# A DeltaNet and MLP-mixer kernel: its steps in another order of issue

## The chip, the cores and the metric

The kernel runs on one NeuronCore of a Trainium2 chip. Its time is the device time of one launch in microseconds (us), from first to last work on that core. Several runs are taken and their median is given; one further execution is recorded by the hardware profiler, and its trace and page are what is read here. Engines are named as the profile names them: PE is the matrix engine (TensorE), PEld its weight load, DVE the vector engine, ACT the scalar engine, POOL is GpSimd, SP the engine that issues the DMAs.

## The reference

Inputs are q, k, v of shape (4, 8, 768, 48), beta (4, 8, 768), and four weight matrices. A recurrence over 768 steps comes first, then an MLP-mixer on its outcome. All is float32.

```
k_n = k / (norm(k, axis=-1) + 1e-6)
for t in range(S):                                  # per batch and head
    y[t]  = q[t] @ state                            # state is 48 x 48
    state = state + beta[t] * outer(k_n[t], v[t] - k_n[t] @ state)
x = y as (B, S, H * D)                              # (4, 768, 384)
h   = relu(x^T @ w_tok1) @ w_tok2                   # 768 -> 256 -> 768, over tokens
u   = x + h^T
out = u + relu(u @ w_ch1) @ w_ch2                   # 384 -> 1536 -> 384, over channels
```

## The kernel before

The recurrence is computed in chunks. A *unit* u is 128 tokens of one batch for all eight heads: 24 units, six to a batch. A *chunk* t is 64 tokens: 48 chunks, twelve to a batch. Inside a chunk the steps become products of matrices, for which a triangular matrix has to be inverted; from chunk to chunk a state of 48 x 48 for each head is handed on, so the chunks of a batch must follow each other. A mixer needs all twelve chunks of its batch.

The work is written as Python generators, each of which issues a few instructions and then yields. One `next` of a generator is called a *step*. The jobs are:

- `k{u}` loads k and q of a unit (`load_kq`, L296): one DMA for k (kpad), one for q (qpad), and either four copies on ACT (first four units) or four more DMAs (`stacked`, L315) for a second layout of k (kst).
- `v{u}` loads v in four DMAs (v_st) and scales it on POOL (L328).
- `p{u}` prepares a unit (`prep`, L344): norms of k, transposes on PE (L376, L392), products p_g (L406), masking by DVE into gm (L412). Its last steps (`to_parts`, L465) hand the unit's triangular blocks to the inversion: by copies on chip for the first six units, by four DMAs into DRAM (n_dram, L479) for the others.
- `i{rnd}` inverts the blocks of two to four units at once (`invert`, L501): units 0 to 3 are round 0, units 4 and 5 round 1, then four at a time and two in round 6. It is a chain of pairs of DVE instructions (L523 a product into sub, L528 the addition to x). From round 2 on x is read from DRAM in its first step (L517) and written to it in its last (w_dram).
- `f{u}` brings the inverted blocks back to gm (`from_parts`, L484).
- `h{u}` (`join_16`, L547; first six units only) and `j{u}` (`join`, L578) put the small inverted blocks together, with PE, ACT and DVE by turns. In `join_16` the four last copies alternate between ACT and DVE (L574).
- `r{t}` is a chunk of the recurrence: `recur_early` (L605) for batch 0, `recur` (L681) for the others. It goes from PE to DVE (L630 or L703, the subtraction of v, into rw_bd), back to PE (p_w), to ACT, to PE (p_s), and DVE writes the next state (L657 or L733, s_bd).
- `m{b}` is the mixer of a batch (L752): p_1 and p_h for the tokens, then in pairs of units p_c (L821) with a relu on ACT (L828), and seven products p_o (L841), each added to the residual xb by DVE (L790). L814 forms sums that save one of eight products.
- `w{j}` loads a piece of a weight matrix and rounds it (`round_weights`, L206) with DVE, ACT and POOL by turns (L221, L226, L233, L235).
- `b` loads beta. `x`, `z` (`keep_warm`, L162) and `y` (`warm_tiles`, L171) are matmuls of zeros that nothing reads.

There is no scheduler: `tc.manual_schedule()` leaves instructions as they are recorded, and the string `order` in the kernel lists 2148 steps by job, `p4*3` being three steps of p4. Each engine gets its instructions in that sequence, and works through them in it; an instruction waits on semaphores for what it reads and for buffers that come free. SP takes DMA issues in the same way. PSUM is shared by three groups of buffers: prep (two), seq (two), mlp (three). v_st has two buffers, kpad and qpad four each, gm room for six units.

The loop at the end of the kernel:

```
for word in order.split():
    name, _, n = word.partition("*")
    for _ in range(int(n or 1)):
        next(jobs[name])
```

Of the kernel before, what the change touches and what calls it, by code (L numbers as in the profile page):

```python
# [10 lines left out]
ALU = mybir.AluOpType  # L11
# [12 lines left out]
def kernel(  # L24
# [39 lines left out]
    nc = tc.nc  # L64
# [56 lines left out]
    for i in range(2):  # L121
        r = slice(C * i, C * i + C)
# [5 lines left out]
    NV = 6  # L128
# [6 lines left out]
    kqts = tiles("kqt", [128, NB, 2, C], NV)  # L135
# [4 lines left out]
    r_bd = w_bd = const.tile([128, NP, 2 * D], FP32, name="rw_bd")  # L140
# [12 lines left out]
    w1 = const.tile([128, NCH, DTOK], FP32, name="w1")  # L153
    w2 = const.tile([128, NDH, S], FP32, name="w2")
# [113 lines left out]
    vsts = {}  # L268
    ksts = {}
    rounds = [[0, 1, 2, 3], [4, 5]]  # L270
    while rounds[-1][-1] < NU - 1:
        u = rounds[-1][-1] + 1
# [68 lines left out]
    def gm_of(u):  # L341
        return gmb[:, (u % NV) * NB : (u % NV + 1) * NB]
# [88 lines left out]
    for n in (QB * RU * NB, RU * NB * QB):  # L431
# [5 lines left out]
        out=low16,  # L437
        in_=ident.rearrange("s (q t) -> s q t", t=HB)[:, :, QB:HB],
# [242 lines left out]
    def recur(t):  # L681


        b, c = divmod(t, NQ)
        u, cc = divmod(t, 2)
        assert t == len(steps)
        steps.append(t)
        gm, kqt, v_st = gm_of(u), kqts[u % NV], vsts[u]
        if c == 0:
            xbs[b] = mlp_pool.tile([128, NCH, DM], FP32, name="xb", tag="xb")  # L690
        y = xbs[b][C * cc : C * cc + C, c // 2].rearrange("s (p n) -> s p n", p=NP)
# [4 lines left out]
        if c > 0:  # L696
            p_q = ps_seq([128, NP, 2 * D], "p_q")
            for p in range(NP):
                nc.tensor.matmul(p_q[:, p], kqt[:, 2 * p + cc], s0[:, p])  # L699
            yield  # L700
            for i in range(2):
                r = PAR[i ^ cc]
                nc.vector.tensor_tensor(  # L703
                    out=r_bd[r, :, ends[i ^ cc]], in0=p_q[lo, :, ends[i]],
                    in1=v_st[r, :, cc], op=ALU.subtract,
                )
        else:
            for r, e in zip(PAR, ends):
                nc.gpsimd.tensor_copy(out=r_bd[r, :, e], in_=v_st[r, :, cc])
        yield  # L710

        assert u in scaled and u in joined
# [194 lines left out]
    jobs["z"] = keep_warm(4)  # L907
    jobs["y"] = jobs["Y"] = warm_tiles()
    order = """
    k0 b y w10 y x k0*5 y*2 w10*3 p0*3 b*2 w1*3 k1*2 p0*2 w10 p0 w1 p0*3 x*2 p0 k1*4  # L910
    p1 w3 x w3*3 v1 w1 p0 k2 v1 k2*2 k3 x*3 p1*2 k2 v1 p0 k2 p0 k2 p1*2 p2*2 k3 v0*2
    p1*4 z x p1 x p2*3 k3*3 p1 k4 v1 w6 k3 w3 p0*2 p1*2 k4 p2*4 v0 k4 y*2 p3*2 p0 w6
    p1 p2*4 p3*4 y*2 w6 y k4*2 p4 p3 v0 p4 k5*2 w2 k5 p1 p3*2 p4 p2*4 p1 y*2 p1 k5*2
    p3*6 p0 p3*2 i0*2 v0 z k6 k7 k6 i0 k5 p4*2 i0*2 k6*2 w6 i0 k4 w6 w2 i0 w2 i0 y
    w18*2 v1 i0 z y*3 x p4*4 y*2 p4 x*2 p4*2 z x*2 y*3 k8 x z x*3 k7*4 k8 z*3 k8*4
    i0*3 w8 p4 i0*4 p5 w2 k6 w2 i0 w18 w13 w8 p5 p4*3 y*3 h0*2 k7 f0*2 w18 f0 p5 f0
    p5 h1*2 z p6 h2*2 f2*2 p5 h0*4 j0 h0 y*2 p5 f2*2 x p6 w18 k6 w8 p4 j0*2 p5*3
    h2*5 j0*2 y*2 w8 r0*2 f1*4 w8 w13*2 p5*4 r0*3 h1*2 r0 h1 p5*3 h1 p5 h1 w13 x*2
    r1*2 y*2 r1*2 p7 r1 h3 k9 w11 k9 w11 j1*2 i1 k9*2 i1 w11 w0 i1 r1 j2 r1 h3 z i1
    j1*2 r1 w11 f3 w11 v2 i1 j1 r2*2 j2*2 i1 r2 p7 w0 p6*4 w0 r2*2 y j2*2 r1 i1 r2*2  # L920
    f3*2 p8 f3 x*3 r2*2 r3*2 i1 w13 v2 r3 x r3*2 x w5 i1 v2 k9 w5 i1 w0*2 h3 v2 p6*2
    h3 p6*2 w5 r3 y v2 r3*3 h3*3 y*2 k9 w5 k10 i1*2 j3 r4 k10 p6 w14*2 r4 w14*2 w5
    p8 p6 r4*2 i1 w14 r4 w17*2 y p7 r4 j3 p8 i1 w17 y w17 y*2 j3 r4*3 k10*2 p6 r5 i1
    r5*2 j3*2 w17 w9*2 i1 p7 r5*2 i1 p7*2 w16 v4 w16 v4 p6 w9 p7*4 v4*2 y w16 r5*3
    y*2 z r5 v3 v4 v3*2 w9 v3 k11 p6*2 p9 p7 v3 p7*2 r6*3 p8 w9 h4*2 r6 w16 r6 p6
    w27*2 w16 p8*3 w27 k11 p8 w7 r6 p8 r6*2 f4 r6 p9*2 h5*2 x f4 p9 r7*2 w7*2 p8
    w27*2 r7 k12 k10 f4 p10 f5 p8 w7 p8*2 f5*2 r7 f4 z p7 f5 w24*2 p9*2 y*3 p7 w24
    h4 r7*2 v5 p7*2 p8 w26 w7 p9*2 z w4 h4 w24 h4*2 r7*2 h4 p10 p9 p10 p9 w24 w26*3
    p8 j4 p9*3 y w4*2 p8 y r7 x j4*2 w26 p10 h5*4 r8*2 j4 v5 w28 v5 y k13 j4 h5 j5
    r8*3 y*2 p9*4 w28 w27 w28 p8 w4 r8 p10 r8 w29 r8*2 w4 w28 w29 r9*3 j5 w29 v5 r9  # L930
    i2 y i2 y i2 w28 i2 r9*4 k11*2 v5 i2*2 j5*2 r10 j5 r10 k12 i2 z r10*2 k13 y k11
    y r9 k13 w15*2 i2 w15 k13 v7 w22 p11 w29*2 r10*4 y*3 r10 p10*2 i2 w22 i2 w22 i2
    r11 y k11 y k13*2 y*2 k12 y*2 k10 r11*3 k12 i2 w15*2 i2*2 w22 w19*2 w22 r11 v7*3
    i2 w19 k12 i2 w12*2 i2 w12 i2 v6 i2 z w19*2 w12*2 r11*2 m0*3 p10*2 w21 v6*3 w23
    i2*5 m0*3 z m0 i2*2 m0 i2 m0*2 i2*2 m0*4 x p10 w25*2 i2*2 w25 i2 p11 w21*2 w25*2
    w31 p11 w23 z w23 w21*2 w23 f7 f6 w31*2 f6*3 f9 k12 f7 f9 w23 v6 v7 m0*2 w31 m0
    f7 m0*2 j6 w31 p12 m0*3 w20 f8 j6 f8*3 j6 m0 j6*2 r12 m0 r12 w29 p12*2 j7 w25 j7
    p13 f7 w20 p11*2 j8 r12*2 j7 f9 j7 p11 w20*2 j8 k14 f9 k14 j7 j8 w25 r12 w20 x
    r13 p10 r13*2 p10*2 r13 w32 w27 w32*2 m0 j9 w32 r13*2 w32 m0 r14 p12*3 m0 p10*4
    v8*2 j8*2 r14*2 p11 w30 j9 w23 p11 r14*2 j9 m0*2 w30 p11 v8 w30 p11 w30 j9*2 r14  # L940
    w30 r15 k14*2 p13 r15 w29 p11*3 k14 k16 r15*2 v8 m0 k16 k14 p12*3 w33 w25 w33
    w27 m0 r15 w33 k16 p12 k16 p11*2 p13 p12 p11 r15 v10 k15*5 p12 v10*2 v8 w33 m0
    w23 r16 p12 w33 p12 v10 p12*3 p13 m0 p11 k16 p13*5 r16 w23 w31 m0 w29 w31 w33*2
    r16 p14 p13*4 w33 p13*4 w31 i3 r16*3 m0*3 p14*2 r17*2 p14 m0*2 v9*2 m0 i3*2
    p14*2 i3 v9*2 i3 r17 p14 k17*2 i3*3 m0*2 k17*2 m0 i3*2 p14 m0 v9 r17*2 i3*3 r17
    v10 p15*2 m0 i3*2 p14*2 i3*2 m0 k17 k18 i3*4 p15 p16 m0*5 r18 m0*2 i3 m0*3 r18
    m0 i3 m0*4 i3*2 k15 i3*3 r18*2 k18*2 p14 k18*2 i3*4 r18*2 m0*5 r19*2 f10*4 m0
    f11*2 p14*5 m0 v11*2 r19 k16 m0 p16*2 j10 m0*2 f13 v11 f11 p15*2 f12 f13 r19*3
    j10 m0 j10 m0*2 p17*2 j11 p15*4 r20*2 p15 j10 f12*2 j10 j11 k19*2 m0 p16 r20 p18
    j11 p18 k17 v11 f11 r20 j12 p15*2 v11 r20*2 m0 r21 j11 p15 j12 j11 p14 j12 f13  # L950
    r21*2 p16 m0 r21 p15*2 k19 p15*2 v12*5 r21 p17 p16*2 k19 p16 p17 r21 m0*2 r22*2
    p16 p18 p16*3 r22 f13 k19*2 p16 p18 p16*2 f12 r22 p16 m0*2 r22*2 m0*3 r23*2
    p17*5 m0 j12*2 r23*2 k21*2 m0 v13 r23 p17*3 v13 p17 v13*2 r23 j13 p16 v13 m0*4
    k21*2 k20*3 k21*2 p17*2 k20 p17*2 m0*2 k18 m0*5 k20 i4*2 m0*2 i4*2 k20 i4*2 m0
    i4*2 m0*2 i4 p18 j13 i4*2 r24*2 p20 r24 m1 r24*2 m1 i4*3 r25*2 i4 v14 p18 i4*2
    m1*2 p18*3 m1 i4*3 m1 j13*2 r25 m1 j13 r25*2 i4 r25 m1*2 i4*3 m1 v14*3 m1 r26*2
    p20 m1*3 r26*2 p18*2 i4*3 v14 i4 p19*3 p18 i4*3 k22 i4 m1 r26 f15 f14*2 r26
    f16*2 f15 f14 k22*2 f17 p20 m1*3 r27 p20 r27 p19 j14 m1 p19 p18 m1*8 p19 m1*4
    j14 f15*2 k22 r27 p18*2 k22 j15 f17*2 j14 v15*2 k22 f14 r27 m1*2 r27*2 j14*2 j15
    r28*2 m1*2 j15 f16 f17 r28 j15 m1 r28*3 p19*2 m1 j16 v15*2 j15 r29*2 p19*3 r29  # L960
    p19*2 m1 p20 r29*2 p22 r29 j16 m1 r30 j16 k23*3 p18 j17 p22 p18 f16 p19*2 m1*2
    p20*2 v15 p20*2 r30*3 v16*2 j16 p21*2 j17 r30*2 p21 j17 v16*3 m1*2 r31 p19 k23*2
    p21 p20 j16 p20 r31*3 p23 p20 v17*4 p20*2 m1 p21 m1 p20*3 p23 p21*2 r31*2 p21*2
    v17 p23*2 m1 p21 r32 p22*2 p21 m1*2 p21*4 p19 p21*2 j17 r32*2 m1 r32*3 k23 m1
    r33*2 m1*2 r33*2 i5 p22*2 j17 m1 r33 i5 m1 i5*3 r33 i5 m1*2 i5*4 p22*2 i5*2 p22
    m1*2 p22 i5 v18*5 m1*3 r34*2 i5*2 p22 m1*2 p22 r34 i5*2 m1*2 i5 p23 r34 m1 r34
    i5 r34 i5 m1*2 i5*2 m1*3 i5*3 p22*5 i5 m1*2 i5*6 m1 f18*4 f19*4 r35*2 f21 v19
    m1*5 f21 m1*4 f21*2 j18 m1 j18 p23 j18 r35*2 m1*5 p23 v19 m1 p23 r35 j18 p23 j19
    f20 j19 f20 m1 f20 m1*2 j19 m1*8 j20 m1 j18 v19 r36*3 p23*6 r36*2 p23*2 r35 m2*2
    r37 i6 r37 i6*5 m2*4 r37 v20 m2 i6 r37 f20 r37*2 v20*2 v19 v20 m2*2 i6*2 m2 i6  # L970
    m2*2 i6 v19 m2*2 r38 j20 j19*2 m2 r38*3 m2 j21 i6 r38 i6*3 m2 r38 i6 j20 r39*2
    m2*2 i6*2 r39 i6*3 v21 r39 v21*2 i6*2 m2 r39 j20*2 m2 i6*2 v21 i6*2 j21*2 i6 v20
    i6*2 r39 i6*2 m2*10 r40*2 f23 m2 f23*2 f22 m2 r40*2 f22*2 m2 v21 m2*3 r40*2 f23
    m2*2 r41 j21*2 f22 j22*2 r41*3 v22 m2*3 r41 j23 v22 m2*3 r41 m2*16 r42 m2*2 j22
    r42*2 m2*2 r42*3 m2*2 v22*3 r43*2 j22 j23 r43 m2*2 r43*3 v23 m2*2 r44*2 j22
    v23*4 m2 j23*2 r44*2 m2*2 r44*2 m2 r45 j23 m2 r45*2 m2 r45*3 m2*2 r46*2 m2 r46
    m2 m3 r46*3 m3 r47*2 m2*2 r47*2 m3 m2 m3 r47*2 m3 m2 m3*2 m2*3 m3*4 m2 m3 m2*3
    m3 m2*4 m3 m2*6 m3*88 x
    """
    for word in order.split():  # L980
        name, _, n = word.partition("*")
# [34 lines left out]
```

## Time and profile before

| | us |
|---|---|
| median of five runs | 722.23 (715.38 to 725.86) |
| the profiled execution | 717.61 |
| its span, first to last instruction | 715.8 |
| PE busy | 688.2 (96%) |
| weight load busy | 600.3 (84%) |
| DVE busy | 438.2 (61%) |
| ACT busy | 242.0 (34%) |
| POOL busy | 98.0 (14%) |

The page cuts the span into 40 slices of 17.9 us and gives the busy share of each engine in tenths (9 is 90% or more), and the granted PE clock in tenths:

```profile
PE   8699898999999999999999999999999999999998
PEld 6468777757889999987999898978999986989987
DVE  6987989798899974568555695258723332221212
ACT  7546656424652324213244312113212231021110
POOL 2221353223231012200012100000000000000000
PEclk9987999799999999999999999999999999999999
```

A float32 matmul of the program shows as two records in the trace, a transpose as one. Matmuls overlap each other in the trace, so the sum of their lengths says less than the distance from the start of one to the start of the next. "Idle before" in the list of groups is the time in which the engine had nothing to run ahead of an instruction; a wait is put down to what came last.

### The profile page before, as it was taken

The page shows a single profiled execution, that of the slowest core. Times are in us where ns is not written, and L with a number is a line of the kernel's source. Part 1 is how long each engine was busy: PE and PEld are TensorE (multiplying, and loading weights), DVE is VectorE, ACT ScalarE, POOL GpSimd, SP SyncE. Part 2 cuts the span into 40 slices and gives each one's busy share as a digit, 9 for nine tenths or more (in the row PEclk, how much of TensorE's full clock was granted, in tenths as well). Part 3 has the DMA queues.
Part 4 walks back from the last instruction along what each step waited for, and adds up shares of the span by engine and source line. Part 5 has one row for each costly group of instructions (what it writes and reads, how often), then busy time and mean ns, then how long its engine had stood idle before and what let it go on. Part 6 is the DMA issues. An engine that isn't in the chain of part 4 may idle for free.

```text
span 715.8 us, 18631 instructions
## 1 busy us (share of the span) xinstructions
PE 688.2 (96%) x7784; PEld 600.3 (84%) x7784; DVE 438.2 (61%) x1163; ACT 242.0 (34%) x569; POOL 98.0 (14%) x118
## 2 busy tenths in 40 slices
PE   8699898999999999999999999999999999999998
PEld 6468777757889999987999898978999986989987
DVE  6987989798899974568555695258723332221212
ACT  7546656424652324213244312113212231021110
POOL 2221353223231012200012100000000000000000
PEclk9987999799999999999999999999999999999999
DMA  9752465843554244431322203020110100000000
GB/s 182 154 114 56 101 147 128 172 125 81 119 105 95 35 100 74 79 79 24 74 47 60 65 1 82 12 64 12 31 34 1 34 1 1 23 0 23 1 23 22
DMA packets 146756, 46.14 MB, mean 64 GB/s; under 512 B 138064, under 2 KB 141136, under 8 KB 146672
## 3 DMA queue, kind: packets, MB, share of 16 engines
q1 hardware_dynamic: 146672, 44.95, 28.8%
q8 instruction: 61, 1.00, 0.6%
q14 instruction: 23, 0.19, 0.1%
HBM read 35.49 MB, written 9.44 MB: 63 GB/s over the span
## 4 chain that ended last, share of the span: by engine, by line
PE 76%; DVE 12%; DMA 5%; SPq 3%; issue 2%; ACT 1%; DVEq 0%; ACTq 0%
PE p_c L821 25%; PE p_o L841 21%; PE p_q L699 4%; PE p_s L725 4%; PE p_w L715 4%; PE p_h L772 3%; PE p L759 3%; PE p_g L406 3%; PE p_x L598 2%; DVE x L528 2%; PE p_warm L166 2%; DMA x<-n_dram 2%; PE p_z L589 1%; DVE sub L523 1%; DMA d<-in_moe_w_ch_dram 1%
## 5 line engine op out<-in xcount | busy, mean ns | idle before, releaser
L821 PE MATMUL p_c<-u_t,wc 128*128 128x256 f32 x864 | 196.4, 381 | 0.0
L821 PEld LDWEIGHTS p_c<-u_t,wc 128*128 128x128 f32 x864 | 160.7, 190 | 21.7 <-issue 0.5
L841 PE MATMUL p_o<-wc,r 128*128 128x192 f32 x720 | 126.7, 328 | 1.5 <-DVE xb L790 0.9
L841 PEld LDWEIGHTS p_o<-wc,r 128*128 128x128 f32 x720 | 117.1, 190 | 3.5 <-DVE xb L790 1.2
L828 ACT ACTIVATE r<-p_c 128x512 f32<-128x512 f32 x72 | 42.8, 596 | 184.9 <-PE p_c L821 184.9
L790 DVE TENSOR_TENSOR xb<-xb,p_o 128x192 f32<-128x192 f32 x84 | 29.4, 350 | 75.0 <-PE p_o L841 75.0
L523 DVE TENSOR_TENSOR sub<-x 128x84 f32<-128x84 f32 (+24 forms) x178 | 59.1, 332 | 12.3 <-DMA x<-n_dram 8.6
L528 DVE TENSOR_TENSOR x<-x,sub 128x84 f32<-128x84 f32 (+24 forms) x178 | 62.6, 352 | 6.1
L814 DVE TENSOR_TENSOR s<-r 128x384 f32<-128x384 f32 x24 | 13.7, 570 | 74.1 <-ACT r L828 74.1
L841 PE MATMUL p_o<-wc,s 128*128 128x192 f32 x288 | 50.7, 327 | 0.0
L233 POOL TENSOR_TENSOR w_f<-w_f,d 128x384 uint32<-128x384 uint32 (+1 forms) x34 | 34.0, 1000 | 115.8 <-DVE w_f L226 52.5
L841 PEld LDWEIGHTS p_o<-wc,s 128*128 128x128 f32 x288 | 46.8, 190 | 0.0
L718 ACT COPY rw_bd<-p_w 64x192 f32<-64x192 f32 x72 | 22.4, 311 | 54.5 <-PE p_w L715 53.0
L328 POOL TENSOR_TENSOR v_st<-v_st,nrm 128x384 f32<-128x384 f32 x24 | 20.9, 875 | 144.4 <-DMA v_st<-in_v_dram 53.2
L412 DVE TENSOR_TENSOR gm<-p_g,mb 128x512 f32<-128x512 f32 x48 | 31.3, 683 | 12.6 <-POOL gm L397 6.1
L385 POOL TENSOR_TENSOR mb<-mask_c,cs 128x512 f32<-128x512 f32 x20 | 21.5, 1073 | 125.5 <-DVE gm L412 67.7
L699 PEld LDWEIGHTS p_q<-s_bd,kqt 128*128 128x128 f32 x264 | 33.6, 191 | 3.7 <-issue 1.2
L699 PE MATMUL p_q<-s_bd,kqt 128*128 128x96 f32 x264 | 34.3, 273 | 1.5 <-DVE s_bd L733 1.5
L725 PEld LDWEIGHTS p_s<-rw_bd,gm 128*112 128x112 f32 x288 | 33.0, 178 | 3.0 <-issue 0.5
L703 DVE TENSOR_TENSOR rw_bd<-p_q,v_st 64x192 f32<-64x192 f32 x66 | 23.1, 350 | 20.2 <-PE p_q L699 15.1
L759 PE MATMUL p<-xb,w 128*128 128x384 f32 x96 | 34.6, 501 | 0.0
L725 PE MATMUL p_s<-rw_bd,gm 128*112 128x96 f32 x288 | 34.2, 262 | 0.0
(111 smaller groups left out, 965.6 us busy)
## 6 DMA issues: line engine op xcount, KB each, us to landing
d<-in_moe_w_ch_dram SPq DMA_DIRECT2D x24, 384.0 KB, 3.6
kpad<-in_k_dram SPq DMA_DIRECT2D x24, 192.0 KB, 3.5
qpad<-in_q_dram SPq DMA_DIRECT2D x24, 192.0 KB, 3.7
v_st<-in_v_dram SPq DMA_DIRECT2D x96, 48.0 KB, 2.6
out_dram<-xb SPq DMA_DIRECT2D x24, 192.0 KB, 1.9
kst<-in_k_dram SPq DMA_DIRECT2D x80, 48.0 KB, 2.8
n_dram<-gm SPq DMA_DIRECT2D x72, 32.0 KB, 1.8
gm<-w_dram SPq DMA_DIRECT2D x72, 32.0 KB, 2.1
```

Source lines behind the costliest of these rows:

```text
L233: nc.gpsimd.tensor_tensor(out=f, in0=f, in1=lo, op=ALU.add)
L412: nc.vector.tensor_tensor(out=blocks(gm)[:, :, cc, 0 : 2 * C].rearrange("s p (two n) -> s p two n", two=2), in0=p_g[cc], in1=mb[:, :, cc, ...
L523: nc.vector.tensor_tensor(out=tmp, in0=y[:, :, 0:s, s : s + 1].to_broadcast([n, k, s, w]), in1=y[:, :, s : s + 1, s + 1 : m].to_broadcast( ...
L528: nc.vector.tensor_tensor(out=y[:, :, 0:s, s + 1 : m], in0=y[:, :, 0:s, s + 1 : m], in1=tmp, op=ALU.add,)
L699: nc.tensor.matmul(p_q[:, p], kqt[:, 2 * p + cc], s0[:, p])
L715: nc.tensor.matmul(p_w[0 : C + 1, p], gm[:, 2 * p + cc, 0 : C + 1], r_bd[:, p])
L725: nc.tensor.matmul(p_s[0 : C + D, p], gm[:, 2 * p + cc, C:], w_bd[:, p])
L759: nc.tensor.matmul(p_1[dh], piece_of(w1, c, 0)[:, dh * 128 : (dh + 1) * 128], xb[:, c], start=(c == 0), stop=(c == NCH - 1),)
L790: nc.vector.tensor_tensor(out=xb[:, c, e], in0=xb[:, c, e], in1=p, op=ALU.add)
L821: nc.tensor.matmul(p_c[:, k], piece_of(wc1, cb, f * 128)[:, f * 128 : (f + 1) * 128], u_t[:, cb], start=(cb == 0), stop=(cb == NCB - 1),)
L828: nc.scalar.activation(r2[:, m], p_c, ACTF.Relu)
L841: nc.tensor.matmul(p, a[:, m], wc2[:, m, j], start=(start and m == 0), stop=(m == NM - 1), skip_group_check=True,)
```

## The change

The string `order` is replaced by another. It has the same steps, and as many of each job, but for one `z` less and one `x` more. Both versions begin in another way, place the loads, preparations and inversions differently among the mixers' steps, and end alike. The description given with it is that the order was searched with both nominal and lengthened operations.

The function `recur` is edited in one thing: it looks up `vsts[u]` where v is used, not at its first step, so that a recurrence's first step may stand ahead of the job that makes v's buffer.

```diff
-        gm, kqt, v_st = gm_of(u), kqts[u % NV], vsts[u]
+        gm, kqt = gm_of(u), kqts[u % NV]
...
-                    in1=v_st[r, :, cc], op=ALU.subtract,
+                    in1=vsts[u][r, :, cc], op=ALU.subtract,
...
-                nc.gpsimd.tensor_copy(out=r_bd[r, :, e], in_=v_st[r, :, cc])
+                nc.gpsimd.tensor_copy(out=r_bd[r, :, e], in_=vsts[u][r, :, cc])
```

From the order, first its beginning, then the stretch from i2's end to r12, the stretches around i3 and i4, those with v16 and v20, and the end:

```diff
-    k0 b y w10 y x k0*5 y*2 w10*3 p0*3 b*2 w1*3 k1*2 p0*2 w10 p0 w1 p0*3 x*2 p0 k1*4
-    p1 w3 x w3*3 v1 w1 p0 k2 v1 k2*2 k3 x*3 p1*2 k2 v1 p0 k2 p0 k2 p1*2 p2*2 k3 v0*2
+    w2*3 w3 y x w3*2 w2 k0 b x w3 k1 v1 x*4 k2 k0*4 x*2 w2 w10 k0 p0 v1 w3 p0 k1*3 y
+    x k1*2 k3 z v1 p1 b p1 p0 b p0*6 p1 w10 x p0 p1 w10 k2*5 p2 p1*2 p0*3 p2 p1*4 z
...
-    i2*5 m0*3 z m0 i2*2 m0 i2 m0*2 i2*2 m0*4 x p10 w25*2 i2*2 w25 i2 p11 w21*2 w25*2
+    v6 m0 v6 p12 m0 i2 m0 i2*2 m0 i2 m0*2 i2 w23 i2 w23 i2 w25*3 i2*2 p10*4 m0*2 z
...
-    r16 p14 p13*4 w33 p13*4 w31 i3 r16*3 m0*3 p14*2 r17*2 p14 m0*2 v9*2 m0 i3*2
-    p14*2 i3 v9*2 i3 r17 p14 k17*2 i3*3 m0*2 k17*2 m0 i3*2 p14 m0 v9 r17*2 i3*3 r17
-    v10 p15*2 m0 i3*2 p14*2 i3*2 m0 k17 k18 i3*4 p15 p16 m0*5 r18 m0*2 i3 m0*3 r18
+    r17*2 i3*2 m0*2 v9*3 r17*2 k16 i3 m0 k16 m0 v10 i3*2 k16 r18*2 v10*3 i3*3 p16*2
+    m0*4 k15 k17 i3*21 k15 k17*2 r18*2 p14 m0*2 i3 m0 f10 r18*2 v10 f10*2 f13 p14*2
...
-    p17*5 m0 j12*2 r23*2 k21*2 m0 v13 r23 p17*3 v13 p17 v13*2 r23 j13 p16 v13 m0*4
-    k21*2 k20*3 k21*2 p17*2 k20 p17*2 m0*2 k18 m0*5 k20 i4*2 m0*2 i4*2 k20 i4*2 m0
+    r23 p17 j13 r23 p16*2 p17 m0*2 v13*5 r23*3 p17*4 p20 m0 j13 k20 k21*2 j12 k21
+    p20 p18 m0 p18 m0 p17 m0*6 p17*3 i4*5 j12 m0 p18 i4 m0*3 i4*2 k21*2 m0*2 i4*3
...
-    p20*2 v15 p20*2 r30*3 v16*2 j16 p21*2 j17 r30*2 p21 j17 v16*3 m1*2 r31 p19 k23*2
+    m1 r30 p19*2 r31*2 p20 v17*3 p20*4 m1 p20 m1 p20 v16 p21*3 j16 r31 j16 r31 p21
+    m1 r31*2 p21*2 v16*2 p20 v16*2 p21*4 r32*2 p21*3 m1*2 i5 j17*2 r32*2 p23*2 m1*2
...
-    m2*2 i6*2 r39 i6*3 v21 r39 v21*2 i6*2 m2 r39 j20*2 m2 i6*2 v21 i6*2 j21*2 i6 v20
+    r39*2 j20 j21 r40 m2 j21 j20 j21*2 v20*2 i6 v20*3 r40*3 m2 i6*4 r40*2 i6 m2 r41
...
-    m3 m2*4 m3 m2*6 m3*88 x
+    m3*17 x*2 m3*71
```

## The prediction

> **What bounds the kernel now.** I first split the profiled execution into stretches. The three lines below give the length of a stretch, the busy time of each engine in it with its instruction count, the granted TensorE clock, and the DMA share and rate.
>
> ```profile
> 0.00:160.00 160.00, 139.07 (x3126) 108.66 (x3127) 135.23 (x358) 89.65 (x220) 47.42 (x60) 0.89 0.60 132
> 160.00:260.00 100.00, 98.37 (x963) 87.30 (x962) 89.93 (x237) 39.61 (x93) 21.43 (x23) 1.00 0.39 86
> 260.00:716.00 456.00, 450.79 (x3698) 404.32 (x3696) 213.05 (x570) 112.74 (x256) 29.18 (x35) 1.00 0.16 36
> ```
>
> The columns after the length are PE, weight load, DVE, ACT, POOL. DVE is busy 85% and 90% in the first two stretches, then 47%. PE looks full throughout, but I don't take its busy time at face value. I charge each matmul the spacing it shows when nothing holds it up. The chain of waits has it: six p_c records in 1.30 us (216 ns each), six p_o records in 0.98 us (163 ns), four p records in 1.32 us (about 323 ns by the median start-to-start). Counted so, 864 p_c records are 186 us, 1008 p_o 164 us, 192 p and p_h 62 us, the later recurrences (p_q, p_w, p_s) 79 us; with preparation, joins and the rest the useful work is **601 us**. The warm-keeping matmuls (lines 166, 176) are 36 us more. So 715.8 - 601 = 114.5 us of the span is lost to PE: 91 before 160 us (69 us of useful work done by then), 8 from 160 to 260, 15 after. An order can only win from these.
>
> What holds PE early is DVE. Its waits in the first 160 us (us in total, times, longest) are few and short:
>
> ```profile
> DVE w_f L221 <- DMA d<-in_moe_w_ch_dram: 5.8, 2, 3.9
> DVE gm L574 <- ACT gm L574: 5.3, 6, 2.6
> DVE s_bd L657 <- PE p_s L653: 2.6, 2, 1.4
> DVE sub L523 <- DMA x<-n_dram: 1.1, 1, 1.1
> ```
>
> Late, a single place stands out, in the chain of waits by time (start, us, what). It is i4, an inversion round whose input goes through DRAM:
>
> ```profile
> 303.39 1.68 DMA n_dram<-gm
> ...
> 305.19 5.41 DMA x<-n_dram
> ...
> 310.63 0.20 DVE sub L523
> ...
> 311.04 0.28 DVE xb L790
> ...
> 311.36 0.76 PE p_o L841 x3
> ```
>
> The step's data goes out and back in 7.2 us; DVE, which takes its instructions in order, stands before it; the residual add xb (L790) behind it frees the PSUM bank that PE needs.
>
> **What the Trainium skill says.** "Perfetto Trace Analysis", Identifying the Most-Contended Engine: matmul busy time is a bad measure since matmuls are pipelined; weight-load busy share is better. The trace agrees: PE is 96% busy but weight load 84%, and p_c's mean record is 381 ns where its spacing is 216. The same page, Optimization Strategy: with regimes of different limits, interleave them. Here PE-heavy m0 can't begin before its recurrences. "TensorE: Matmul & The Clock Gate", Part 1: an array that idles gets a lower clock. The trace shows 0.89 in the first 160 us and 1.00 after, so waits there have a second cost. "DMA: Bandwidth & Descriptors", Anatomy of one DMA: most of a small transfer's fixed time is the completion, worst towards HBM; the 1.7 to 3.2 us of the small n_dram writes fit.
>
> **The change, part by part.** No arithmetic is added or removed: per engine both programs have as many instructions (TensorE 4024, DVE 1163, ACT 569, SP 437, POOL 121). One z becomes an x (warm matmul of 512 columns to one of 128: 0.65 us less, in waits anyway: 0). The late reading of vsts only lets a recurrence's first step stand ahead of its v load: 0 by itself.
>
> *a. DVE's lead.* For every matmul that waits for DVE, I sum DVE's work in program order up to what it waits for (each instruction its median by shape, plus the 34 ns that lie between two of them) and subtract PE's useful work ahead of it. PE has lost at least this, plus DVE's own waits. Where the sum peaks, the front ends. Before: 88.5 us, at r19 (DVE 245.7, PE 157.2). It ran at 256.2 us, so DVE's net waits were 10.5 us and PE's loss 99.0. After: 91.1 us, at r20 (DVE 251.3, PE 160.2). Between, the orders are near-twins: at r0 DVE 54.9 before and 55.4 after, at r11's end 148.7 and 143.6, at i2's end 161.7 and 161.9, at i3's load 206.1 and 207.3, PE within 3 us each time. The later peak comes from r18 to r20 moving ahead of m0 work. **+2.6 us.**
>
> *b. The start.* SP now issues w2, w3, k0, b, k1 and so on, where it issued k0, b, w10, k0's q. Before, DVE's first rounding step waited until 6.1 us: w10's DMA was third, issued at 1.85 us, and took 4.2. Now w2 is first, at about 0.74 us, and should land near 4.6. k0 is third: two issues of 0.43 to 0.6 us later, so its four copies on ACT (from 3.77 us before, 0.36 each) and the square end near 7 to 8 us, beside w2's and w3's rounding on DVE. POOL's w2 and w3 adds fall in POOL's idle time. **-1.5 us** (0 to -2.5).
>
> *c. Round trips through DRAM.* Per round, the time from DVE's last mask product (gm, L412) to the inversion's first DVE step is four SP issues (1.4 us), the write (1.7 to 3.2) and the read (3.5 to 5.7): 6.7 to 10. DVE work placed in between, before and after: i2 15.1 and 9.0, i3 6.1 and 7.8, i4 5.3 and 3.3, i5 4.3 and 3.2, i6 2.1 and 3.3 us. i2's SP queue was held up by two further DMAs before, one now; I take its 1.1 us as gone (bounds -1.1 and +1). i3 had 0.5 us and keeps it. i4 to i6 come when DVE has slack, so PE's cover counts: from the p_g matmul to the first one blocked i4 has 13.8 us after against 13.0, and needs 1.5 + 8.4 + 2.2 = 12.1. Before, two v and k DMAs stood in SP's queue between; these are gone. PE's 1.4 us wait there goes. i5 has 25.9 us; i6 16.7 against at most 16.2. **-1.1 and -1.4 us.**
>
> *d. ACT and POOL.* The join_16 copies (L574) made DVE wait 5.3 us. Pairs that follow each other directly on DVE with ACT's copy between: three before, six now; but fewer stand behind other ACT work. Unknown from the trace: taken as 0, bounds -3 and +3.
>
> *e. v loads moved.* Each must pass SP's queue, land (2.6 us) and be scaled on POOL (0.9 us), about 6 us with its issues. DVE work between the release of the buffer and the use is at least 8 us in all; v16's last issues stand behind p20's write with 3.8 us left, at a place where DVE has 40 us in hand. Cost 0; cover gone, 1 to 2 us of DVE that PE doesn't see.
>
> *f. The tail.* m3's last 71 steps follow alone in both (88 before); 3.6 us from the last matmul to the end of the store stay. 0.
>
> Sum: 717.6 (profiled execution: 715.8 span and 1.8 around it) + 2.6 - 1.5 - 1.1 - 1.4 = 716.2. The median of the five runs, 722.2, stands 4.6 above the profiled one, so the forecast is 716.2 + 4.6, about **720.5 us**.
>
> **Rivals.**
> *Parity* (the forecast): the above; with d and the bounds of b and c, 715 to 727. For it: the twin sums. Chance 0.42.
> *Fewer queue waits, faster*: an order that was laid out for longer operations as well should leave room where the trace shows DVE late although the sum left no gap: L574's 5.3 us, the w_f loads' 5.8, s_bd's 2.6, and 15 us of small PE waits after 260 us. If half of the 13.7 and a third of the 15 go, 720.5 - 6.9 - 5 + 2.6 (b and c not counted twice) = 711. For it: of DVE's waits on other engines that leave under 1 us of room, the orders have 9 and 4 between DVE's 50th and 90th us. Against: from the 200th to the 300th it is 7 and 8. Chance 0.36.
> *DVE falls behind between r17 and r20, slower*: the lead stays above 89 us over 60 us of PE work now, where it touched 88 before; any DVE wait there is paid in full. i3's 21 steps now stand in one row with r18 and the m0 adds behind. If its read takes the 5.7 us that i2's took (round trip 9.8 against 7.8 of cover: +2.0), the L574 pairs cost +3, i2 doesn't gain (+2.1) and b gives nothing (+1.5): 720.5 + 8.6 = 729. It decides once new DVE waits before r20 exceed some 7 us. Chance 0.22.
> That the move changes nothing because PE is full holds only after 260 us, and is part of parity.
>
> **Numbers.** About 1% (7.2 us) is what a measurement of this kernel can tell from no change; its runs spread over 10 us. Range 706 to 732: the fast rival with another 5 us, the slow one with 3 more. Chances: faster by over 1% 0.36, within 1% 0.42, slower 0.22, one for each case.
>
> **What would show it.** a: r19 or r20's p_w near 256 to 260 us, after about 160 us of useful PE work. b: DVE's first w_f step before 5 us. c: no PE stop at i4 and no idle DVE ahead of i2's first step. d: the wait L574 on ACT under 8 us. Wrong, if PE's loss after 260 us departs from 15 us by over 4, or if DVE's waits up to r20 are not 8 to 13 us.

## The result and the profile after

| | before | after |
|---|---|---|
| median, us (lowest to highest; runs) | 721.81 (713.65 to 728.56; 77) | 716.09 (711.09 to 719.77; 42) |
| ratio, 95% interval | | 0.9947 [0.9932, 0.9963] |
| the profiled execution, us | 717.61 | 714.41 |
| its span, us | 715.8 | 712.6 |

The new order is faster by 0.5%, which is less than the 1% taken as "no change". The ratio counts only runs within 1.5% of the fastest of their kernel, which leaves out 29 of before's 77 and none of after's; over all runs the means are 722.04 and 715.79 us, a ratio of 0.991. The new order also spreads less: the standard deviation of its runs is 2.2 us, against 3.8. The profiled executions differ by 3.2 us, the medians by 5.7; before's profiled execution was one of its quicker ones.

First, two lines of the page of after: the busy times, and the group of the inversion's products (columns: busy, mean ns of one, idle time ahead of them and its releaser).

```profile
PE 683.4 (96%) x7784; PEld 595.6 (84%) x7784; DVE 427.1 (60%) x1163; ACT 241.7 (34%) x569; POOL 97.0 (14%) x118
...
L523 DVE TENSOR_TENSOR sub<-x 128x84 f32<-128x84 f32 (+24 forms) x178 | 59.0, 332 | 4.3 <-DMA x<-n_dram 0.3
```

DVE runs the same 1163 instructions and is busy 427.1 us, not 438.2. So the same instructions got shorter, by 11 us in all: something the prediction has no term for. The inversions wait 0.3 us for their DRAM read.

The same three stretches as before, in the same columns:

```profile
0.00:160.00 160.00, 136.19 (x3126) 105.19 (x3127) 131.37 (x365) 90.52 (x221) 47.29 (x61) 0.88 0.61 131
160.00:260.00 100.00, 98.82 (x1098) 88.31 (x1096) 87.02 (x241) 42.90 (x101) 21.19 (x23) 1.00 0.42 91
260.00:713.00 453.00, 448.35 (x3572) 402.06 (x3564) 208.68 (x558) 108.33 (x247) 28.57 (x35) 1.00 0.16 35
```

In the first 160 us DVE finishes 365 instructions in 131.4 us of busy time, where it finished 358 in 135.2. With the prediction's count of useful PE work (601.3 us in both), the loss of PE runs as follows, in us at the given time:

| loss of PE at | 60 | 120 | 160 | 200 | 262 | the end |
|---|---|---|---|---|---|---|
| before | 44.0 | 72.9 | 91.2 | 95.0 | 99.2 | 114.5 |
| after | 42.7 | 70.8 | 86.5 | 93.6 | 96.6 | 111.3 |

Of the 3.2 us, 2.6 are there by 262 us, and 0.6 come later. The time was won in the front, where DVE leads.

Now DVE's waits of after in the first 160 us (us in total, times, longest):

```profile
DVE gm L574 <- ACT gm L574: 7.9, 9, 3.8
DVE s_bd L657 <- PE p_s L653: 3.3, 2, 2.0
DVE w_f L221 <- DMA d<-in_moe_w_tok_dram: 2.3, 2, 1.4
DVE ksum L355 <- ACT ksq L352: 2.3, 2, 1.3
```

They aren't fewer. The w_f loads give back 2.1 us (5.8 to 2.3 and, further down the list, 1.4), but the L574 pairs cost 7.9 us, not 5.3.

To see what DVE's time is made of, I add up its instructions to the subtraction in r19 (L703), where its lead peaked before: each at the median of its shape, then how much longer than that it took ("lengthening"), then the gaps over 60 ns ("waits"). The rest, about -8 us, is the few ns by which each overlaps the next. (r19's p_w, which waits for this subtraction, starts at 256.2 us before and 251.9 after.)

| up to r19's L703, us | ends at | at medians | lengthening | waits |
|---|---|---|---|---|
| before | 255.7 | 224.2 | 17.5 | 21.7 |
| after | 250.2 | 223.6 | 8.2 | 26.5 |

The work is equal, lengthening falls by 9.3 us, waits take 4.8 back, and r19 comes 5.5 us earlier.

What lengthens an instruction shows in the groups by line. The columns are min/median/max ns, first and last start, shape. Before:

```profile
L253 DVE TENSOR_TENSOR wc<-wc x24: 312/350/985, 124.6 to 216.4; 128x192 f32<-128x192 f32 x24
```

```profile
L362 DVE TENSOR_SCALAR nrm<-nrm x24: 129/163/792, 9.2 to 394.4; 128x8 f32<-128x8 f32 x24
```

And after:

```profile
L362 DVE TENSOR_SCALAR nrm<-nrm x24: 120/164/172, 10.3 to 417.6; 128x8 f32<-128x8 f32 x24
```

One shape, one median, and a maximum of three to five times that; in the new order L362 has none. The timeline of before, around the longest L253 (start, us, what):

```profile
204.74 0.95 POOL L328 TENSOR_TENSOR v_st<-v_st,nrm 128x384 f32<-128x384 f32 x1
...
204.92 0.98 DVE L253 TENSOR_TENSOR wc<-wc 128x192 f32<-128x192 f32 x1
```

POOL's product is under way when DVE's subtraction starts. It ends at 205.69, DVE's at 205.90. The Trainium skill says so in "SBUF — State Buffer", Who interferes with whom: a DVE instruction with both inputs in SBUF contends with a GpSimd instruction that reads SBUF, and whichever issues first holds the shared ports for its whole length. The trace agrees: 0.98 us where 0.35 is usual.

### The profile page after: what moved, and what is told of

It reads as the page before. It is cut to its first block, busy times and chain, and to the rows that moved or that the text cites. A ratio compares the mean times of both kernels' runs of the same rounds, so it can differ in the third digit from the quotient of the medians.

```text
span 712.6 us, 18616 instructions
## 1 busy us (share of the span) xinstructions
PE 683.4 (96%) x7784; PEld 595.6 (84%) x7784; DVE 427.1 (60%) x1163; ACT 241.7 (34%) x569; POOL 97.0 (14%) x118
## 4 chain that ended last, share of the span: by engine, by line
PE 76%; DVE 16%; DMA 4%; issue 2%; ACT 2%; SPq 0%; POOL 0%; DVEq 0%; POOLq 0%; ACTq 0%
PE p_c L821 23%; PE p_o L841 21%; PE p L759 5%; PE p_q L699 4%; PE p_s L725 4%; PE p_h L772 4%; PE p_w L715 3%; DVE x L528 3%; DVE sub L523 3%; PE p_x L598 2%; PE p_z L589 2%; PE p_g L406 2%; DVE gm L412 1%; PE p_warm L166 1%; DVE w_f L226 1%
## 5 line engine op out<-in xcount | busy, mean ns | idle before, releaser
L814 DVE TENSOR_TENSOR s<-r 128x384 f32<-128x384 f32 x24 | 13.4, 557 | 91.0 <-ACT r L828 91.0
L528 DVE TENSOR_TENSOR x<-x,sub 128x84 f32<-128x84 f32 (+24 forms) x178 | 61.3, 345 | 6.1
L523 DVE TENSOR_TENSOR sub<-x 128x84 f32<-128x84 f32 (+24 forms) x178 | 59.0, 332 | 4.3 <-DMA x<-n_dram 0.3
L718 ACT COPY rw_bd<-p_w 64x192 f32<-64x192 f32 x72 | 22.5, 312 | 70.8 <-PE p_w L715 57.0
L233 POOL TENSOR_TENSOR w_f<-w_f,d 128x384 uint32<-128x384 uint32 (+1 forms) x34 | 33.6, 993 | 92.1 <-DVE w_f L226 51.5
L733 DVE TENSOR_TENSOR s_bd<-s_bd,p_s 48x192 f32<-48x192 f32 x60 | 21.4, 357 | 28.7 <-PE p_s L725 27.9
L412 DVE TENSOR_TENSOR gm<-p_g,mb 128x512 f32<-128x512 f32 x48 | 31.1, 683 | 4.1 <-PE p_g L406 3.0
```

The lines of the kernel that those rows point to most:

```text
L233: nc.gpsimd.tensor_tensor(out=f, in0=f, in1=lo, op=ALU.add)
L412: nc.vector.tensor_tensor(out=blocks(gm)[:, :, cc, 0 : 2 * C].rearrange("s p (two n) -> s p two n", two=2), in0=p_g[cc], in1=mb[:, :, cc, ...
L523: nc.vector.tensor_tensor(out=tmp, in0=y[:, :, 0:s, s : s + 1].to_broadcast([n, k, s, w]), in1=y[:, :, s : s + 1, s + 1 : m].to_broadcast( ...
L528: nc.vector.tensor_tensor(out=y[:, :, 0:s, s + 1 : m], in0=y[:, :, 0:s, s + 1 : m], in1=tmp, op=ALU.add,)
```

## The experiments

The expectations use these names. **FRONT**: the gain arises up to r19's end. **BACK**: after it. **START**: within the front, it is the first stretch, up to the end of i0's chain, which in the traces ends at 43.9 us after and 48.3 before. **CHAIN**: within the front, what comes between i0 and r19. **COLLIDE**: it is the fewer DVE instructions that stand behind a POOL instruction. All ratios are to the kernel before, as it ran beside each of these kernels on the same chip. Its median there was 723.96 us beside front_new, back_new and the two kernels named no_add, 723.18 beside after_again, start_new, start_old and after_more_pool, 724.30 beside after_pool_memset, w10_first and join_act, and 724.96 beside join_act_more. Medians of different rows should be read as distances to these.

### Which part of the order

Four kernels cut the two orders at one point and join the first part of one to the other's sequence for all that is left. after_again is after, unchanged.

front_new, the new order to r19's end (1185 steps), then the old one:

```diff
     p14*3 p17*2 m0*3 j10 r19 j11 j10 p16 p14 m0*2 r19*2 p15 r19
-    j10*2 j11*2 r20*2 f12 f13 p15 f13 ...
+    z x k18*5 v11*2 m0*3 v11 p15*2 ...
```

back_new, the old order to r19's end (1193 steps), then the new one:

```diff
     ... f11 p15*2 f12 f13 r19*3
-    j10 m0 j10 m0*2 p17*2 j11 p15*4 ...
+    k17 f11 p17*2 j10 j11 j10 p16 p14 j10*2 ...
```

start_new, the new order to i0's end (227 steps), then the old one; start_old, the old order to i0's end (238 steps), then the new one:

```diff
     ... k6*2 k8*2 v0 k6 k8 i0
-    h2*2 h0 w1 p5 w6 x h1 h0 f0 ...
+    w1*2 v0 v1 v0*3 w6 w18 v1 k7 z ...
...
     ... i0*3 p5 w2 k6 w2 i0
-    w18 w13 w8 p5 p4*3 y*3 h0*2 ...
+    x*2 p4 y h2*2 h0 p5 x h1 h0 f0 ...
```

front_new: 

> The changed order up to the end of r19, then the remaining steps in the sequence of the order before. Theory FRONT (what is won is won before about 260 us, where DVE sets the pace): time within 1.5 us of the changed kernel, near 717, ratio to before 0.993 to 0.997. Theory BACK (won later, at the inversions' trips through DRAM and in small waits of PE): within 1.5 us of before, near 721. Split evenly: near 719.

back_new: 

> The order before up to the end of r19, then the remaining steps in the sequence of the changed order. FRONT: near the kernel before, 720 to 722, ratio 0.998 or more. BACK: near the changed kernel, 716 to 718. Its trace should show a loss of PE of about 99 us at r20 in either case; after that 11 us under FRONT, under 10 under BACK.

start_new: 

> The changed order up to the end of i0's chain (about 44 us), then the remaining steps in the sequence of the order before. Theory START (most of the gain is made before i0 ends: 48.3 us before, 43.9 after, and handed on down the recurrences): time 4 us or more under the kernel before, within 2 us of the changed one. Rival CHAIN (it is made between r0 and m0's first products): within 2 us of the kernel before.

start_old: 

> The order before up to the end of i0's chain, then the remaining steps in the sequence of the changed order. START: within 2 us of the kernel before, i0 ending near 48 us. CHAIN: within 2 us of the changed kernel.

after_again: 

> The changed kernel itself, for a comparison on the same chip and a second trace. 5 to 7 us under the kernel before. At the end of i0's chain near 44 us (before: 48.3), at r11 between 141 and 148 us as the granted clock happens to fall.

| | median, us (runs) | ratio, 95% interval | i0's chain ends, us | r19's p_w, us |
|---|---|---|---|---|
| after_again | 717.47 (22) | 0.9959 [0.9935, 0.9982] | 44.0 | 252.1 |
| front_new | 718.45 (14) | 0.9921 [0.9892, 0.9949] | 44.2 | 257.8 |
| back_new | 734.42 (6) | 1.0143 [1.0092, 1.0193] | 48.8 | 267.5 |
| start_new | 718.26 (22) | 0.9958 [0.9929, 0.9986] | 44.2 | 255.8 |
| start_old | 718.71 (22) | 0.9936 [0.9912, 0.996] | 48.9 | 258.2 |

By its runs front_new keeps the whole gain without any of the new back (5.5 us below before's median, as forecast by FRONT), so FRONT stands. In its trace PE loses 14.4 us after 262 us, against 15.3 before and 14.7 after: the new back brings nothing to speak of. The trace doesn't show the gain in the front, though. It is of the longest of its 14 runs (720.45 us), and r19's p_w comes at 257.8 us, 5.9 later than in after, whose steps to there are the same. Counted as above, its lengthening is within 0.5 us of after's; its waits are 5.8 us more.

back_new can't be read as BACK alone. Its steps up to r19 are before's, yet r11's p_w starts at 155.3 us, where before has 145.2. The windows show why. Before, then back_new, each from 60 to 160 us (the third column from the end is the granted clock):

```profile
60.00:160.00 100.00, 90.70 (x2230) 73.12 (x2227) 87.38 (x228) 55.78 (x140) 33.23 (x37) 0.89 0.55 127
```

```profile
60.00:160.00 100.00, 92.34 (x2204) 77.08 (x2199) 76.02 (x209) 52.57 (x134) 29.35 (x31) 0.72 0.52 116
```

With the same instructions the clock was 0.72, not 0.89 (the last section shows where the two part). DVE got through 209 of them, not 228, and was idle 24 us instead of 13. In this stretch its two chief waits on PE (s_bd for p_s, rw_bd for p_k) rose from 3.0 to 11.0 us:

```profile
DVE s_bd L657 <- PE p_s L653: 7.0, 4, 2.3
DVE rw_bd L630 <- PE p_k L626: 4.0, 3, 1.6
```

By 160 us PE's loss is 8.8 us larger (100.0 against 91.2); a further 9.0 is lost after 160, in the part where the two orders are spliced. So one trace of a front is a draw, to some 10 us at r11, and the runs have to decide. But all six runs of back_new (728.75 to 737.19 us) lie above nearly all of before's beside it (717.1 to 729.91): the spliced order is slower in itself, which neither theory foresaw, and the kernel says nothing on where the gain lies.

By the runs start_new and start_old each come out some 0.5% below before, and neither can be told from the whole change. If the gain lay in one part alone, one of the two would have stood near 1: each theory is right about one of the kernels and wrong about the other. Over all runs on this chip the means are 722.60 us for before, 719.79 for start_new, 718.57 for start_old and 717.44 for after_again, with standard errors of 0.4 to 0.8. That is 2.8 and 4.0 of the 5.2 us, as if each part had a share; more than that isn't shown. i0's earlier end, by some 4 us, holds in every trace of the new start and in none of the old; but start_old has a gain without it. Nor is the gain tied to collisions alone: start_new's lengthening to r19 is only some 2 us below before's, where start_old's is 6 below and after's 9.

### Is it the first load?

```diff
-    k0 b y w10 y x k0*5 y*2 w10*3 p0*3 ...
+    w10 k0 b y*2 x k0*5 y*2 w10*3 p0*3 ...
```

w10_first, the order before with w10's load issued first: 

> The kernel before with one step moved: w10's load is issued ahead of k0 and beta. Step b of the prediction: DVE's first rounding step starts near 4.7 us where it started at 6.1, k0's copies up to 0.5 us later. If the start's gain (4.4 us at the end of i0) comes from that first wait, i0 ends 1 to 1.5 us earlier and the time falls by up to 1.5 us; if it comes from what follows (collisions and order up to 30 us), i0 ends within 0.7 us of 48.3.

722.97 us in 22 runs, 0.9977 [0.9944, 1.0011]. DVE's first rounding step in before, in w10_first, and then in after (timeline; in brackets the idle time ahead of it and its releaser):

```profile
6.09 0.36 DVE L221 TENSOR_SCALAR w_f<-d 128x384 uint32<-128x384 uint32 x1 [3.89 <-DMA d<-in_moe_w_ch_dram]
```

```profile
4.26 0.36 DVE L221 TENSOR_SCALAR w_f<-d 128x384 uint32<-128x384 uint32 x1 [2.06 <-DMA d<-in_moe_w_ch_dram]
```

```profile
3.56 0.29 DVE L221 TENSOR_SCALAR w_f<-d 128x256 uint32<-128x256 uint32 x1 [1.36 <-DMA d<-in_moe_w_tok_dram]
```

It comes 1.8 us earlier than before's 6.09, and yet i0's chain ends at 49.5 us, against before's 48.3 (up to here w10_first's clock is before's 0.90; later it is lower, so I read no further). That misses both forecasts. The wait moved to the next place: ksum (L355) waits 3.23 us for ACT's square of k and starts at 8.44 us, against 8.07 in before. An early wait that goes is not a gain by itself here. In the account of before and after up to i0's end, the 4.4 us are 1.3 of less DVE work ahead, 2.3 of less lengthening, 1.0 of shorter waits, less 0.2 of the rest.

### Collisions with POOL

Four kernels change how often POOL runs. Two leave out POOL's addition in the rounding of weights (L233); two add POOL work behind each L233, on a tile that nothing reads any more.

```diff
 before_no_add, after_no_add:
-        nc.gpsimd.tensor_tensor(out=f, in0=f, in1=lo, op=ALU.add)
 after_more_pool:
+        for _ in range(3):
+            nc.gpsimd.tensor_tensor(out=mask_f, in0=mask_f, in1=mask_f, op=ALU.mult)
 after_pool_memset:
+        for _ in range(6):
+            nc.gpsimd.memset(mask_f, 0.0)
```

before_no_add: 

> The kernel before without POOL's addition in the rounding of weights (L233); it leaves out the low bits of the weights. 34 us of POOL work and nothing of PE or DVE go. Theory COLLIDE (DVE instructions that overlap one of POOL's last until it ends, 15.8 us of lengthening up to 262 us in the profile before, 6.4 in the one after): lengthening drops to about 7 us, time falls by 5 to 9 us. Rival HIDDEN (the lengthening falls where DVE would have waited anyway): under 2 us.

after_no_add: 

> The changed kernel without POOL's addition in the rounding of weights (L233); it leaves out the low bits of the weights. COLLIDE: lengthening falls from 6.4 to about 3 us up to 262 us, time falls by 2 to 4 us to about 713, and the distance to the kernel before without that addition closes to under 2.5 us. HIDDEN: the distance stays near 5.7 us.

after_more_pool: 

> The changed kernel with three further POOL products on an unused tile (128x128 each, some 0.4 us each) after every addition of the rounding (L233): about 40 us more POOL work, nothing read by anyone. Theory COLLIDE: DVE lengthening up to 262 us grows from about 12 to over 18 us and the time by 4 us or more. Rival HIDDEN (a longer DVE instruction falls into what DVE would have waited): under 2 us more.

after_pool_memset: 

> A control for after_more_pool: instead of three products, six memsets of the unused tile (128x128, 0.21 us each in the trace) follow every addition of the rounding on POOL. As much POOL time, in the same places, but these read no SBUF. If the 7 us of after_more_pool came from DVE instructions held by POOL (COLLIDE[...]), the lengthening up to 262 us stays under 16 us and the time within 3 us of the changed kernel. If they came from POOL's own work being late (mb, gm, v, the next rounding), the time rises by 5 us or more here too.

| | median, us (runs) | ratio, 95% interval | lengthening to r19, us | waits | r19's L703 ends |
|---|---|---|---|---|---|
| before | 721.81 (77) | 1 | 17.5 | 21.7 | 255.7 |
| before_no_add | 720.59 (22) | 0.9951 [0.9927, 0.9976] | 10.2 | 27.5 | 255.1 |
| after | 716.09 (42) | 0.9947 [0.9932, 0.9963] | 8.2 | 26.5 | 250.2 |
| after_no_add | 714.89 (6) | 0.9875 [0.9824, 0.9927] | 2.8 | 31.5 | 250.4 |
| after_more_pool | 724.53 (22) | 1.0033 [1.0008, 1.0058] | 19.2 | 24.0 | 258.5 |
| after_pool_memset | 722.2 (22) | 0.9989 [0.9963, 1.0015] | 12.3 | 27.9 | 255.6 |

The two additions occupy POOL alike. Their groups on the page, first of after_more_pool, then of after_pool_memset (busy us, mean ns of one, idle before):

```profile
L235 POOL TENSOR_TENSOR mask_f<-mask_f 128x128 f32<-128x128 f32 x102 | 45.9, 450 | 5.3
```

```profile
L235 POOL MEMSET mask_f<- 128x128 f32 x204 | 43.5, 213 | 9.8
```

After_pool_memset has both kinds of POOL work within a microsecond of each other. From its timeline (two lines were added, so L525 and L530 are L523 and L528 of the other kernels):

```profile
132.93 0.99 POOL L235 MEMSET mask_f<- 128x128 f32 x4
133.11 0.18 DVE L525 TENSOR_TENSOR sub<-x 128x30 f32<-128x30 f32 x1
133.32 0.19 DVE L530 TENSOR_TENSOR x<-x,sub 128x30 f32<-128x30 f32 x1
...
133.90 0.21 DVE L525 TENSOR_TENSOR sub<-x 128x58 f32<-128x58 f32 x1
...
134.12 1.02 POOL L233 TENSOR_TENSOR w_f<-w_f,d 128x384 uint32<-128x384 uint32 x1 [0.19 <-issue]
134.15 1.06 DVE L530 TENSOR_TENSOR x<-x,sub 128x58 f32<-128x58 f32 x1
```

Beside POOL's memsets, DVE's products and additions take 0.18 to 0.21 us as ever. 30 ns into POOL's addition, the next takes 1.06 us. Over this whole trace, of the L523 and L528 that started during a memset none of 15 was lengthened; of those that started during a POOL sum or product, all 19. This too agrees with the page named above: a GpSimd instruction that only writes SBUF does not contend with an instruction of two SBUF inputs.

So the memsets are the control, though not a clean one: they make the weights later on POOL without colliding themselves, but their trace still has 4 us more lengthening than after's, from collisions with the other POOL work.

By the ratios they cost 0.30 to 0.42% of the time (0.9989 against after's 0.9959 and 0.9947), about 2.6 us. These ratios are to different sets of before's runs; by medians, each read as its distance to before's beside it, the memsets cost 3.6 us (2.1 below, where after_again is 5.7 below) and the products 7.1 (1.4 above). The expectation had under 3 us if the cost was in collisions and 5 or more if it was in POOL's own lateness, so it doesn't decide: about half of what the products cost comes with the memsets too. The difference of the two ratios, 0.44% (1.0033 less 0.9989), some 3 us of time for 7 us more lengthening, is what can be put down to collisions, with about 0.36% of uncertainty on it.

Taking collisions away gives less: without L233 before's lengthening falls by 7.3 us and its waits rise by 5.8; r19 moves by 0.6 us, the runs by 0.49%, which includes what POOL's addition itself takes. In time before_no_add gained 3.4 us by medians (720.59 against 723.96), between HIDDEN's 2 and COLLIDE's 5. Had collisions been all that parts the two orders, before_no_add would have come near after at r19; it stayed 4.9 us behind (255.1 against 250.2), though its lengthening is within 2 us of after's. And after_no_add's median is 5.7 us below before_no_add's, the distance of after to before, where COLLIDE had it close to under 2.5. (The distance in lengthening, 7.4 us against 9.3, closed little either, so this pair is a weak test.)

What follows: the new order has fewer collisions (shown, 17.5 to 8.2 us), and adding some costs time (shown, if only just: 0.44% with 0.36% of uncertainty). That they are the cause of the 5.5 us at r19, or of the gain in time, is not shown: where they are taken away, most comes back as waits. The expectation of COLLIDE was too simple in treating lengthening as time. The cause of the gain stays open in part.

### The copies of join_16

```diff
-            on = nc.vector.tensor_copy if i in EARLY_DVE else nc.scalar.copy
+            on = nc.scalar.copy
```

This is the new order, with the four last copies of join_16 all on ACT. join_act: 

> The changed kernel with all four last copies of join_16 (L574) on ACT, where two of four are on DVE. Twelve DVE instructions of 0.29 us go, and with them DVE's 7.9 us of waits for ACT's copies between them. If DVE's waits in the front cost time one for one, 3 to 8 us less than the changed kernel; if the recurrences' chain sets the pace there, under 2 us either way, or slower by the 0.3 us that each copy is later.

join_act_more, the same kernel again: 

> The same kernel as join_act (the changed order, all four last copies of join_16 on ACT), in more runs, since six left its ratio uncertain. If DVE's waits for ACT's copies (7.9 us before 160 us) are paid for at the end, most of them should come back as time: ratio to the kernel before 0.985 to 0.990, against 0.9947 for the changed order. If DVE merely waits elsewhere instead, as join_act's trace showed (other waits took their place, r19 at 251.9 us), the ratio stays at 0.993 to 0.997.

| | median, us (runs) | ratio, 95% interval |
|---|---|---|
| join_act | 716.36 (6) | 0.9897 [0.984, 0.9955] |
| join_act_more | 713.34 (6) | 0.9866 [0.9808, 0.9924] |

DVE's longest waits in the first 160 us of join_act_more:

```profile
DVE t L584 <- ACT gm L574: 5.3, 2, 5.0
DVE s_bd L657 <- PE p_s L653: 5.3, 3, 2.7
```

The wait has moved from the copies to the transposes (L584) that read them. Most of it is PE's: in after's timeline PE stops for 2.27 us within the products (L568) that the copies read, without a reason that the profile shows.

```profile
47.54 0.64 PE L568 MATMUL p_x<-gm,r 32*16 32x16 f32 x54
50.46 0.28 PE L568 MATMUL p_x<-gm,r 32*16 32x16 f32 x10 [2.27 <-issue]
```

r19's p_w is at 253.2 and 252.7 us in the two traces (the expectation's 251.9 is after's), no earlier than after's 251.9. By traces, then, waits took the place of waits; by the ratios it gained, 0.9866 lying in the band expected of a real gain. But that ratio and the 0.9947 it was to be compared with are not to like sets of before's runs. Over all runs the means give 0.9897 and 0.9877 for the two, against 0.9913 for after and 0.9929 for after_again, and the second kernel had six runs again, not more. Whether this version is better than after by a few tenths of a per cent stays open.

## Why the prediction was right, and where not

The forecast, parity at 720.5 us within 715 to 727, came true at 716.09. It held because its band is 12 us wide: the front came out 2.7 us below its sum, what follows 0.8 above, and the step to the median was 2.9 too large. That they fitted in is luck as much as insight. Step by step:

*a, DVE's lead* (+2.6): the place holds, the size doesn't. Redoing the sum in program order puts its peak, 251.3 us of DVE and 160.2 of PE work, at r20's p_q, which waits for DVE to write the state (L733). Both in the timeline of after:

```profile
255.60 0.73 DVE L733 TENSOR_TENSOR s_bd<-s_bd,p_s 48x192 f32<-48x192 f32 x2 [0.42 <-PE p_s L725]
...
256.53 0.69 PE L699 MATMUL p_q<-s_bd,kqt 128*128 128x96 f32 x4
```

p_q starts at 256.5 us, so DVE's net waits were 5.2 us and PE's loss 96.3. The prediction had 7.9 (10.5 less b's 1.5 and i2's 1.1) and 99.0, and it named net waits outside 8 to 13 us as a sign of being wrong. By that sign this term failed, though the time came out right. The step put **every instruction at the median of its shape in both orders**, and so held constant, inside "net waits 10.5", what an order can change: 17.5 us of lengthening before, 8.2 after, of which waits took 4.8 back. That is 4.5 us less by r19, and most of the 5.3 by which the net waits fell. The maxima of L253 and L362 stood in the trace of before.

*b, the start* (-1.5): DVE's first step at 3.56 us, before 5 as said, and i0's chain ends 4.4 us earlier. The early load alone doesn't do that: w10_first has the load and not the early chain.

*c, the round trips* (-1.1 and -1.4): both places are as foreseen. DVE no longer idles ahead of i2 (0.3 us of DRAM waits for all inversions), and the chain of waits of after runs through i4's place without a DMA:

```profile
291.29 5.38 PE p_c L821 x24
296.67 3.90 PE p_o L841 x24
...
301.00 4.07 PE p_o L841 x25
```

Yet PE's loss after 262 us fell by 0.6, not 1.4: 14.7 against 15.3. That is within the 4 us that would have refuted the prediction.

*d, ACT and POOL* (0, bounds -3 and +3): L574 rose from 5.3 to 7.9 us, just under the 8 named, inside the bounds. That join_act removes this wait and r19 comes no earlier bears out taking it as 0 by the trace; its ratios leave room for a gain.

*e and f* (0): front_new, with before's tail of m3, loses the same after 262 us; nothing in the waits points to v.

*The sum*: 716.2 for the profiled execution against 714.4 measured. (716.2 and 4.6 make 720.8; the prediction wrote about 720.5.) The larger part of the error of 4.4 us lies in adding 4.6 to get to the median: after's median stands only 1.7 above its profiled execution.

*The rivals*: "fewer queue waits, faster" was wrong as put. Waits to r19 rose from 21.7 to 26.5 us; half of 13.7 did not go. Where the traces show room, it is in fewer collisions. In time the result lies midway between the forecast's 720.5 and this rival's 711. "DVE falls behind between r17 and r20" did not happen: DVE's net waits up to r20 fell to 5.2 us. (That r18's p_w came at 225.0 us, not 246.5, is the move itself.)

## What to carry to other kernels

When you sum an engine's work from medians, also look at the maxima by shape: where one shape has a maximum of several times its median, look for what runs on the other engine at that moment, and ask whether the new order changes how often they meet. Don't count a lengthening, or an early wait, as time that will come back: in a front that one in-order engine leads, less of one turned up as more of the other, by half (4.8 of 9.3 us) to four fifths (5.8 of 7.3). And where two traces of the same order differ by 10 us at one place, use the runs for what is gained and the trace only for where. Compare ratios only when they are to the same set of runs.

## What was not expected of the hardware

Nearly all of DVE's lengthening comes from one case: POOL is already running a two-input sum or product, and the DVE instruction works from SBUF to SBUF. In the traces of before, after, after_again and back_new, of those that started so, lengthened were 25 of 28 L523, 28 of 31 L528, 10 of 10 L253, 8 of 8 L226, 15 of 18 L235 and 10 of 14 L814; also 12 of 16 L221 and 7 of 8 L362, which have one input. With an input from PSUM it was none of 53 L412 and 52 L657, and of the reductions L355 none of 24. Where POOL came second, DVE kept its time. In whole traces this case makes up 24.5 of 24.7 us of lengthening before and practically all of 13.3 after (counting what is over 60 ns): it is the 11 us by which DVE's busy time fell.

The granted clock in the first 160 us is another draw, and here one can see what it costs. Before and back_new have the same steps up to r19 and keep within 0.5 us of each other up to 70 us. Then, first before, then back_new (windows; the clock is the third column from the end):

```profile
70.00:80.00 10.00, 10.00 (x287) 8.27 (x281) 9.46 (x30) 7.58 (x22) 3.58 (x4) 1.00 0.32 71
```

```profile
70.00:80.00 10.00, 9.50 (x175) 7.44 (x169) 7.11 (x26) 4.54 (x12) 1.17 (x2) 0.54 0.32 72
```

From 80 to 90 us it is 1.00 against 0.50. In back_new the same 32 records of p_x (L598) take 1.06 us instead of 0.69 from 73.1 us on; DVE's first long wait for PE (p_k, 1.58 us) ends at 76.1, and DVE's 200th instruction comes at 96.3 us, where before has it at 88.2. So the clock fell first and DVE followed, though its own instructions are no longer (L630 takes 0.36 us in both). w10_first, with nearly the same order, has 0.50 from 70 to 90 us and its 200th instruction at 95.5. What decides on the clock is not shown: PE's idle time just before, at 68.5 us, was 0.84 us in before and 0.85 in back_new, so the prediction's second cost of waits isn't seen here. In before's 75 runs beside start_new, a straight line through time and mean clock falls by some 4.5 us for each 0.01. The gain of the change is not a better clock: the runs of after_again have 0.965 in the mean, those of before beside them 0.967.
